# An attention and MLP kernel on one core: other homes for two PSUM banks, the gate inside V's product, four kinds of small work on GpSimd, and new planner values

## The chip, the core and the metric

The kernel runs on one core of a Trainium2 chip. A core has five engines that run their own instruction streams: TensorE (PE) multiplies matrices, VectorE (DVE), ScalarE (ACT) and GpSimd (POOL) work elementwise, and SyncE (SP) issues transfers. They wait for each other by semaphores. The metric is the device time of one execution in microseconds; the figure that counts is the median of several executions.

## The reference

x is 2048 x 512 in bfloat16. Two branches and a gate are computed from it:

```
g  = sigmoid((x * gate_w).sum(-1))
a  = attention of 32 heads of 16 columns (softmax over all 2048 keys) @ wo
h  = gelu(layernorm(x) @ w1), its four column quarters shifted by 1, -1, 2, -2 rows
x1 = x + h @ w2
b  = x1 + gelu(layernorm(x1) @ w3) @ w4          (w3: 512 x 1792)
out = g * a + (1 - g) * b
```

## The kernel before

**The planner.** The Python code that builds the kernel is a planner. It holds a clock for each of TensorE, ScalarE, VectorE and GpSimd (`free`), estimated durations, and queues of work that is ready at a planned time (`post`, `queue`). In its last loop it takes again and again the engine whose next piece can start first, chooses among that engine's pieces by rank, and issues the instruction. The order of instructions on each engine is thus fixed when the kernel is built; on the chip only the semaphores decide when each starts. Numbers such as CREDIT, SLACK and GAP and the table RULES (values for each unit of work, in place of those in USUAL) steer its choices.

**Attention.** A unit is one chunk of 512 queries and four heads: 4 chunks x 8 sets = 32 units of 64 score blocks (4 heads x 16 key tiles), each block 128 keys x 512 queries. A slot is three PSUM banks; two slots alternate. TensorE computes three blocks into a slot (`scores`, line 728), ScalarE takes the exponential of them in one instruction (`expo`, line 1036) into a tile `pt`, and TensorE multiplies these with V into the unit's sums `acc` (`attend`, line 1049). V has a column of ones, so the sums hold the softmax denominators too.

**Blocks without ScalarE.** Some blocks take another way. `wants_whole` decides whether the third bank of a slot (`dsc`) holds such a block. VectorE reads it from PSUM into an int16 tile with a shift and a floor (`dump`, line 927), so that the integers are the bits of a bfloat16 approximation of the exponential. Four blocks of one key tile make a group, 128 x 2048. Four further passes (`shifted`, line 964) add constants to the bits, and all five versions are multiplied with V and summed, which evens the approximation out. The group's tiles are called quad, more and xT after the memory they lie in. MAXD caps the blocks of a unit that go this way, CHAINS the groups under way, NEED says from how near the end of a unit the next unit's blocks are taken, and DLIM how much ready VectorE work forbids a new group. A slot without any exponential (`lone_slot`) can stand ahead of and behind a GELU round and holds up to three such blocks.

**The end of a unit.** `finish_unit` copies the sums to `accsb` (line 1119), sends the denominators through DRAM to spread them, and multiplies with their reciprocals (`scale`, line 1142). There is one `accsb`: the next unit's copy waits for the scaling.

**Jobs.** Between the slots TensorE runs jobs: projections of Q, K and V, the MLP's products and the output, in one PSUM bank (`psG`, tag gen) beside the unit's sums (`psA`, tag acc). A credit, raised with every slot, limits them. `q_proj` makes a unit pair's queries: the product is copied from PSUM into two versions, each with half of the columns set to zero by `mask` (line 287). `v_proj` makes half of V's heads for one key tile (copy in line 309), `gates` the gate's sums as one-column products (line 398). `norm` makes layernorm's normalised tiles (line 350). GELU rounds run on ScalarE and need another function table, so that tables are loaded twice for each round.

**Zero products.** Where TensorE would be idle for longer, `fill` multiplies a zero matrix into the open sums, which changes nothing in them.

**The start.** Lines 118 to 145 issue the first loads and prepare constants: GpSimd clears tiles and makes `ident`, `identf` and `minus`, VectorE sums `ident` to `mask` and scales it. Then x's first chunk is transposed on TensorE and copied to `xT` by VectorE and ScalarE (lines 1276 to 1284).

Of the kernel before, what the change touches and what calls it, by code (L numbers as in the profile page):

```python
# [32 lines left out]
def kernel(  # L33
# [21 lines left out]
    VK = 7  # L55
# [39 lines left out]
    wkv = wshare.tile([P, KT, 2 * D], BF16, tag="wshare", name="wkv")  # L95
# [11 lines left out]
    mask = const.tile([P, 2], F32, name="mask")  # L107
    pick = const.tile([P, 4], F32, name="pick")
# [33 lines left out]
    for a in range(2):  # L142
        nc.vector.tensor_reduce(out=mask[:, a:a + 1], in_=idv[:, a], op=ALU.add, axis=AX.XY)
    nc.vector.tensor_scalar(out=mask[:], in0=mask[:], scalar1=QS, scalar2=None, op0=ALU.mult)
# [7 lines left out]
    for j in range(4):  # L152
        for a in range(2):
# [8 lines left out]
    USUAL = {"NEED": 28, "AHEAD": 16, "HURRY": 14, "DLIM": 0.9, "MANY": 5, "PTS": 4, "CHAINS": 5, "MAXD": 16}  # L162
# [34 lines left out]
    state = {"n": 0, "gen": 0, "young": True, "mm": 0, "sp": 0.0, "before": True, "after": False, "aside": 0.0, "kind": "", "t": 0.0, "piece": 0.0,  # L197
             "credit": 0.0, "mixable": 0, "done": False, "ending": False, "acc": 0.0, "accsb": 0.0, "slot": 0, "outs": 0, "bank": 0}
    asides = deque()
    at = {}  # L200
    banks = {0: 0.0, 1: 0.0, 2: 0.0}

    port = {"vector": 0.0, "pool": 0.0}

    def dma(t, own, count=1):

        state["sp"] = max(state["sp"], t) + own * count
        return state["sp"]  # L210

    def post(engine, rank, cost, fn, ready=0.0, shared=False):

        state["n"] += 1
        queue[engine].append((rank, state["n"], cost, fn, ready, shared or engine == "pool"))

    def all_at(*keys):
        return lambda: max(at[k] for k in keys) if all(k in at for k in keys) else None

    def bank_of():
        return state["gen"] % 3 if state["young"] and state["slot"] < EARLY - 1 else 0

    def gen(name, dtype=F32):
        b = bank_of()
# [5 lines left out]
        return psG.tile([P, CH], dtype, tag="gen", name=name)  # L232
# [46 lines left out]
    def q_proj(c, G):  # L279
# [4 lines left out]
        def fn(end):  # L284
            qT = qpool.tile([P, 2, CH], BF16, tag="qT", name="qT")
            qTs[(c, G)] = qT
            nc.vector.tensor_tensor(out=qT[:], in0=ps[:].unsqueeze(1).to_broadcast([P, 2, CH]),
                                    in1=mask[:].unsqueeze(2).to_broadcast([P, 2, CH]), op=ALU.mult)
            at["q", c, G] = end

        evac(1.23, fn)
        yield MM

    def v_proj(t, half):
# [97 lines left out]
    def gates(c):  # L392
# [3 lines left out]
        for j in range(4):  # L396
# [4 lines left out]
            if j < 3:  # L401
                yield 0.2
# [345 lines left out]
    def scores(start):  # L748
# [21 lines left out]
        if mine:  # L770
            blocks = blocks[:2]
# [695 lines left out]
```

## Time and profile before

| | |
|---|---|
| median of 3 runs | 815.23 us (812.69 to 815.72) |
| the profiled execution | 814.83 us, its span 812.9 us |
| TensorE's mean granted clock | 0.987 |
| busy: PE, VectorE, ScalarE, GpSimd | 768.2, 739.5, 778.4, 16.5 us |

The span goes from the first to the last instruction. A row of a group view gives line, engine, operation, output and input tiles with their shapes and a count, then the busy time in us, the mean of one in ns, and the engine's idle time ahead of these instructions with what ended it. A row of a timeline gives start and duration in us. A row of waits gives the total in us, how often, and the longest.

### The profile page before, as it was taken

The numbers are of one execution on the slowest core, as the hardware profiler recorded it, in microseconds if no ns is written. First come the engines' busy times: TensorE is split into PE (matmuls) and PEld (weight loads), VectorE is DVE, ScalarE is ACT, GpSimd is POOL, SyncE is SP. The second block draws the span as 40 slices with busy tenths as digits, with TensorE's granted clock in tenths as the row PEclk, the third lists the DMA queues.
The fourth block names the chain that finished last, engine by engine and source line by source line (L and its number), as shares of the span: only waits on it lengthen the run. The fifth ranks groups of instructions, "written<-read, shape, count | busy, mean of one in ns | idle before, by whom it ended". The sixth has DMA issues, their size and how long they took to land.

```text
span 812.9 us, 24041 instructions
## 1 busy us (share of the span) xinstructions
PE 768.2 (95%) x10308; PEld 265.5 (33%) x10308; DVE 739.5 (91%) x1293; ACT 778.4 (96%) x726; POOL 16.5 (2%) x46
## 2 busy tenths in 40 slices
PE   8999999999999999989999999999999999999997
PEld 4333333233433333332333333333233333323333
DVE  5899989799689999998999997799987999999897
ACT  6999999999899999998999999999999999999996
POOL 3100000000000000000000000000000000000000
PEclk9999999799999999998999999999999999999999
DMA  9600033101200014000100011100020000000101
GB/s 191 193 20 15 11 77 33 44 19 41 44 5 18 17 59 91 9 18 15 43 14 13 25 39 31 29 9 16 19 57 16 8 31 17 23 19 19 31 13 40
DMA packets 52307, 29.05 MB, mean 36 GB/s; under 512 B 36713, under 2 KB 47721, under 8 KB 52201
## 3 DMA queue, kind: packets, MB, share of 16 engines
q1 hardware_dynamic: 51240, 27.00, 13.8%
q8 instruction: 80, 1.31, 0.7%
q10 hardware_dynamic: 960, 0.52, 0.2%
q14 instruction: 27, 0.21, 0.1%
HBM read 17.17 MB, written 2.35 MB: 24 GB/s over the span
## 4 chain that ended last, share of the span: by engine, by line
ACT 51%; PE 26%; issue 18%; DVE 4%; DMA 1%; POOL 1%; SPq 0%; DVEq 0%; ACTq 0%; POOLq 0%
ACT pt L1036 48%; PE acc L1049 10%; PE stage L728 7%; PE ps L237 2%; PE stage L237 2%; PE ps_y L237 1%; DVE quad L927 1%; PE acc L237 1%; ACT g2T L1014 1%; DMA xT<-in_A_x_dram 1%; ACT L1036 1%; ACT g2T L1017 1%; PE ps_q L237 1%; DVE quad L964 1%; PE ps_o L237 1%
## 5 line engine op out<-in xcount | busy, mean ns | idle before, releaser
L1036 ACT ACTIVATE pt<-stage 128x1024 bf16<-128x1024 f32 (+1 forms) x687 | 729.0, 1219 | 18.3 <-PE stage L728 13.6
L728 PE MATMUL stage<-qT,kT 32*128 32x512 bf16 (+2 forms) x1640 | 270.6, 382 | 32.7 <-ACT pt L1036 26.7
L927 DVE TENSOR_SCALAR quad<-dsc 128x512 int16<-128x512 f32 x300 | 200.5, 687 | 12.2 <-PE dsc L728 10.4
L728 PEld LDWEIGHTS <-kT 32*128 32x128 bf16 x2072 | 86.1, 91 | 275.7 <-issue 241.4
L964 DVE TENSOR_SCALAR quad<-quad 128x2048 int16<-128x2048 int16 x248 | 165.2, 685 | 4.5 <-PE acc L1049 4.2
L728 PE MATMUL dsc<-qT,kT 32*128 32x512 bf16 x432 | 165.9, 387 | 0.0
L1049 PE MATMUL acc<-pt,vp 128*17 128x512 bf16 (+3 forms) x1616 | 157.2, 383 | 3.3 <-DVE accsb L1119 2.7
L1049 PEld LDWEIGHTS <-vp 128*17 128x17 bf16 (+1 forms) x3896 | 86.1, 90 | 147.8 <-issue 109.2
L1049 PE MATMUL acc<-quad,vp 128*17 128x512 bf16 x1556 | 132.6, 388 | 0.3 <-DVE quad L964 0.2
L237 PE MATMUL ps<-w,g2T 128*32 128x512 bf16 x896 | 69.2, 381 | 0.0
L927 DVE TENSOR_SCALAR more<-dsc 128x512 int16<-128x512 f32 x79 | 52.7, 686 | 7.2 <-PE dsc L728 6.5
L237 PE MATMUL ps_y<-xnT,w 128*32 128x512 bf16 x704 | 55.1, 386 | 0.1
L237 PE MATMUL acc<-wq,zero 128*32 128x512 bf16 x596 | 51.1, 390 | 0.0
L237 PEld LDWEIGHTS <-w 128*32 128x32 bf16 x1152 | 29.3, 96 | 30.8 <-issue 12.9
L927 DVE TENSOR_SCALAR xT<-dsc 128x512 int16<-128x512 f32 x53 | 35.1, 686 | 2.7 <-PE dsc L728 2.3
L1049 PE MATMUL acc<-more,vp 128*17 128x512 bf16 x380 | 37.2, 388 | 0.1
L1049 PE MATMUL acc<-xT,vp 128*17 128x512 bf16 x344 | 32.6, 383 | 0.0
L964 DVE TENSOR_SCALAR more<-more 128x2048 int16<-128x2048 int16 x39 | 26.6, 685 | 1.5 <-PE acc L1049 1.4
L1119 DVE COPY accsb<-acc 128x512 f32<-128x512 f32 x31 | 21.3, 688 | 6.5 <-PE acc L1049 5.8
L237 PEld LDWEIGHTS <-g2T 128*32 128x32 bf16 x896 | 20.5, 95 | 19.9 <-issue 10.2
L237 PE MATMUL stage<-xnT,w 128*32 128x512 bf16 x448 | 25.1, 379 | 0.5 <-ACT pt L1036 0.5
L964 DVE TENSOR_SCALAR quad<-more 128x2048 int16<-128x2048 int16 x37 | 25.3, 687 | 0.1
(114 smaller groups left out, 543.2 us busy)
## 6 DMA issues: line engine op xcount, KB each, us to landing
bcs<-rec_d SPq DMA_DIRECT2D x31, 256.0 KB
w<-in_B_w_dram SPq DMA_DIRECT2D x2, 1792.0 KB
out_dram<-ot SPq DMA_DIRECT2D x15, 128.0 KB
x_sb<-in_A_x_dram SPq DMA_DIRECT2D x14, 128.0 KB
oT<-oT SPq DMA_DIRECT2D x112, 16.0 KB
w<-in_B_w_dram SPq DMA_DIRECT2D x2, 512.0 KB
wkv<-in_A_wqkv_dram SPq DMA_DIRECT2D x1, 512.0 KB
wo_all<-in_A_wo_dram SPq DMA_DIRECT2D x8, 64.0 KB
```

Source lines behind the costliest of these rows:

```text
L237: nc.tensor.matmul(out[j:j + 32, :], lhsT=lhsT[:, j:j + 32], rhs=rhs, tile_position=(0, j), **kwargs)
L728: nc.tensor.matmul(out, lhsT=kT[G][32 * j:32 * j + 32, cc, o:o + P], rhs=qTs[(c, G)][32 * j:32 * j + 32, a, lo:hi], start=True, stop=True, ...
L927: nc.vector.tensor_scalar(out=bits[:, r, :], in0=dsc[:], scalar1=SHIFT, scalar2=LOWEST, op0=ALU.add, op1=ALU.max)
L964: nc.vector.tensor_scalar(out=tiles[to], in0=tiles[base], scalar1=STEPS[i] - (STEPS[0] if base else 0.0), scalar2=None, op0=ALU.add)
L1014: nc.scalar.activation(out=part, in_=part, func=ACT.Gelu_apprx_tanh)
L1017: nc.scalar.activation(out=dst, in_=stages.pop(k)[:, 0:len(ms) * CH].rearrange("p (a c) -> p a c", c=CH), func=ACT.Gelu_apprx_tanh)
L1036: nc.scalar.activation(out=pt[:, 0:w], in_=stages.pop(k)[:, 0:w], func=ACT.Exp, scale=LN2 / 128.0)
L1049: nc.tensor.matmul(accs[n][32 * j:32 * j + M, lo:hi], lhsT=lhsT, rhs=p, start=(kt == 0), stop=(kt == NT - 1), skip_group_check=True, tile_ ...
L1119: nc.vector.tensor_copy(out=accsb[:], in_=acc[:])
```

## The change

Six things change. (1) The two banks for sums and for jobs lose their fixed roles: if the job bank is free earlier than the sums' bank, a new unit takes it and the roles are exchanged (`homes`, `swaps`). (2) The gate's weights become a 1025th column of the tile of K's and V's weights, written by GpSimd (`column`); the second half of V's product has 257 columns, and the last is the gate's sum. (3) A dump may take up to three neighbouring blocks (rule WIDE, and slots without an exponential). (4) On GpSimd now run: the two masked versions of the queries (with `ones`, in place of one VectorE pass), the normalised tiles, the scaling of all units but the last three, and the last of a group's four shifts where much VectorE work is ready (BACK). (5) The planner keeps account of TensorE's busy share over the last 3.4 us and adds zero products where it falls under 0.4 (`share`, LOW). (6) A tiny exponential behind each GELU round; values and RULES are new.

The diff, with the RULES, repeated entries of the account and lines that only pass on new arguments left out:

```diff
-    VK = 7
+    VK = 5
...
-    wkv = wshare.tile([P, KT, 2 * D], BF16, tag="wshare", name="wkv")
+    wkv = wshare.tile([P, KT, 2 * D + 1], BF16, tag="wshare", name="wkv")
...
+    ones = const.tile([P, 2], F32, name="ones")
+    small = const.tile([P, 1], F32, name="small")
...
+    nc.gpsimd.tensor_copy(out=ones[:], in_=mask[:])
...
-    USUAL = {"NEED": 28, "AHEAD": 16, "HURRY": 14, "DLIM": 0.9, "MANY": 5, "PTS": 4, "CHAINS": 5, "MAXD": 16}
+    USUAL = {"WIDE": 1, "NEED": 28, "AHEAD": 8, "HURRY": 24, "DLIM": 0.9, "MANY": 3, "PTS": 5, "CHAINS": 6, "MAXD": 16}
...
-    VLIM = 2.0
+    VLIM = 6.0
-    RUN = 9.5
+    LOOK = 0.3
+    BACK = 0.6
+    RUN = 1.5
-    CREDIT = 0.5
-    LATER = 0.4
-    GELU, WTWO = 1.2, 1.0
-    MOST = 16.0
+    CREDIT = 0.35
+    LATER = 0.35
+    GELU, WTWO = 1.0, 1.3
+    MOST = 12.0
-    SLACK = 0.3
-    GAP = 0.3
-    AGE = 2.0
-    ARANK = 3
+    SLACK = 0.25
+    GAP = 0.2
+    AGE = 4.0
+    ARANK = 4
-    TANH = 1.5
+    TANH = 3.0
+    WINDOW = 3.4
+    LOW = 0.4
+    PINCH = 0.2
...
+    busy = deque()
+    def works(a, b):
+        busy.append((a, b))
+        while busy[0][1] < b - 8.0:
+            busy.popleft()
+    def share(t):
+        return sum(min(b, t) - max(a, t - WINDOW) for a, b in busy if b > t - WINDOW) / WINDOW
...
+    homes = {"acc": (psA, "acc"), "gen": (psG, "gen")}
+    def home(kind, dtype, name):
+        pool, tag = homes[kind]
+        return pool.tile([P, CH], dtype, tag=tag, name=name)
...
-            nc.vector.tensor_tensor(out=qT[:], in0=ps[:].unsqueeze(1).to_broadcast([P, 2, CH]),
-                                    in1=mask[:].unsqueeze(2).to_broadcast([P, 2, CH]), op=ALU.mult)
-            at["q", c, G] = end
-        evac(1.23, fn)
+            nc.vector.tensor_scalar(out=qT[:, 0, :], in0=ps[:], scalar1=QS, scalar2=None, op0=ALU.mult)
+            def second(end):
+                nc.gpsimd.tensor_scalar(out=qT[:, 1, :], in0=qT[:, 0, :], scalar1=ones[:, 1:2], scalar2=None, op0=ALU.mult)
+                post("pool", 0, 0.65, first, end)
+            def first(end):
+                nc.gpsimd.tensor_scalar(out=qT[:, 0, :], in0=qT[:, 0, :], scalar1=ones[:, 0:1], scalar2=None, op0=ALU.mult)
+                at["q", c, G] = end
+            post("pool", 0, 0.65, second, end)
+        evac(0.69, fn)
-        yield all_at(("xT", c), "wv")
+        yield all_at(("xT", c), ("wv", half))
-            strips(ps[:, 0:width], lhsT=xT[c][:, kt, o:o + P], rhs=wkv[:, kt, D + half * width:D + (half + 1) * width],
-                             start=(kt == 0), stop=(kt == KT - 1))
+            strips(ps[:, 0:width + half], lhsT=xT[c][:, kt, o:o + P],
+                   rhs=wkv[:, kt, D + half * width:D + (half + 1) * width + half], start=(kt == 0), stop=(kt == KT - 1))
...
-        evac(0.42, fn)
+            if half:
+                nc.vector.tensor_copy(out=g_raw[:, t:t + 1], in_=ps[:, width:width + 1])
+                state["raw"] += 1
+                if state["raw"] == NT:
+                    post("act", 1, 0.1, tanh, end + 0.06)
+        evac(0.42 + 0.12 * half, fn)
...
-                nc.vector.tensor_scalar(out=xn[:], in0=x_sb[t][:], scalar1=mvs[n][:, t, 0:1],
+                nc.gpsimd.tensor_scalar(out=xn[:], in0=x_sb[t][:], scalar1=mvs[n][:, t, 0:1],
-            aside(0.41, normed(t), all_at(("rstd", n, c), "xnfree"), True)
+            post("pool", 1, 0.65, normed(t), all_at(("rstd", n, c), "xnfree"))
...
-    def gates(c):
-        yield all_at("gw", ("xT", c))
-        ps = gen("ps_g")
-        for j in range(4):
-            for kt in range(KT):
-                nc.tensor.matmul(ps[:, j:j + 1], lhsT=xT[c][:, kt, j * P:(j + 1) * P], rhs=gw[:, kt:kt + 1],
-                                 start=(kt == 0), stop=(kt == KT - 1))
-            state["piece"] += 0.2
-            if j < 3:
-                yield 0.2
-        def raw(end):
-            nc.vector.tensor_copy(out=g_raw[:, 4 * c:4 * c + 4], in_=ps[:, 0:4])
-            if c == NC_ - 1:
-                post("act", 1, 0.1, tanh, end + 0.06)
-        def tanh(end):
-            nc.scalar.activation(out=g_t[:], in_=g_raw[:], func=ACT.Tanh, scale=0.5)
-            post("vector", 5, 0.17, affine, end)
-        def affine(end):
-            nc.vector.tensor_scalar(out=g_fin[:], in0=g_t[:], scalar1=0.5, scalar2=0.5, op0=ALU.mult, op1=ALU.add)
-            at["g_fin"] = end
-        evac(0.2, raw)
-        yield 0.3
+    def tanh(end):
+        nc.scalar.activation(out=g_t[:], in_=g_raw[:], func=ACT.Tanh, scale=0.5)
+        post("vector", 5, 0.17, affine, end)
+    def affine(end):
+        nc.vector.tensor_scalar(out=g_fin[:], in0=g_t[:], scalar1=0.5, scalar2=0.5, op0=ALU.mult, op1=ALU.add)
+        at["g_fin"] = end
...
-    def wants_whole(blocks, now, alone=False):
+    def wants_whole(blocks, now, alone=0):
-        heads = {m % 4 for _, m in blocks[:2]}
+        most = alone or rule("WIDE")
+            most = min(most, len(rest))
+            heads = [m % 4 for _, m in blocks[:3 - most]]
-            if fit or k - quad["last"] > 2 or alone:
-                return n, kt, (fit or rest)[0]
+            if len(fit) >= most or k - quad["last"] > 2 or alone:
+                return n, kt, (fit + [j for j in rest if j in heads])[:most]
+        heads = [m % 4 for _, m in blocks[:3 - most]]
...
-                return n, kt, [j for j in range(4) if j not in heads][0]
+                last = heads[-1] if heads else 3
+                return n, kt, [j for j in ((last + d) % 4 for d in (1, 3, 2, 4)) if j not in heads][:most]
...
-        st = old[side].tile([P, (2 if kind else 3) * CH], F32, tag="stage", name="stage")
-        return st, old[side].tile([P, CH], F32, tag="dsc", name="dsc") if kind else None
+        st = old[side].tile([P, (3 - kind) * CH], F32, tag="stage", name="stage")
+        return st, old[side].tile([P, kind * CH], F32, tag="dsc", name="dsc") if kind else None
...
-            blocks = blocks[:2]
+            blocks = blocks[:3 - len(mine[2])]
-            st, dsc = stage(k, bool(mine))
+            st, dsc = stage(k, len(mine[2]) if mine else 0)
...
-        for i in range(3):
-            if i:
-                mine = wants_whole([], start, True)
-            if not mine:
-                break
-            n, kt, j = mine
+        i = 0
+        while mine:
+            n, kt, js = mine
-            rows[j] += 1
-            score(st[:, i * CH:(i + 1) * CH], n, 4 * kt + j)
-            whole(k, st[:, i * CH:(i + 1) * CH], n, kt, j, begin + (rows[j] - 1) * MM + PE_OUT)
+            for x, j in enumerate(js):
+                rows[j] += 1
+                score(st[:, (i + x) * CH:(i + x + 1) * CH], n, 4 * kt + j)
+            whole(k, st[:, i * CH:(i + len(js)) * CH], n, kt, js, begin + (max(rows) - 1) * MM + PE_OUT)
+            i += len(js)
+            mine = wants_whole([], start, 3 - i) if i < 3 else None
+        works(begin, free["pe"])
...
-            nc.vector.tensor_scalar(out=bits[:, r, :], in0=dsc[:], scalar1=SHIFT, scalar2=LOWEST,
+            nc.vector.tensor_scalar(out=bits[:, r:r + wide, :], in0=dsc.rearrange("p (a c) -> p a c", c=CH), scalar1=SHIFT, scalar2=LOWEST,
...
-            nc.vector.tensor_scalar(out=tiles[to], in0=tiles[base], scalar1=STEPS[i] - (STEPS[0] if base else 0.0), scalar2=None, op0=ALU.add)
+            shift = STEPS[i] - (STEPS[0] if base else 0.0)
+            if other:
+                nc.gpsimd.tensor_scalar(out=tiles[to], in0=tiles[base], scalar1=1.0, scalar2=shift, op0=ALU.mult, op1=ALU.add)
+            else:
+                nc.vector.tensor_scalar(out=tiles[to], in0=tiles[base], scalar1=shift, scalar2=None, op0=ALU.add)
...
-                post("vector", rank(), 0.69, lambda end: shifted(end, i + 1), end if i == 0 else room_or_base(i + 1, end), True)
+                work = sum(x[2] for x in queue["vector"] if not callable(x[4]) and x[4] < end + 1.0)
+                to_pool = i == 2 and work > BACK and free["pool"] < end + 1.0
+                state["pool"] = to_pool
+                post("pool" if to_pool else "vector", rank(), 2.0 if to_pool else 0.69, lambda end: shifted(end, i + 1, to_pool), end if i == 0 else room_or_base(i + 1, end), True)
...
-            free["act"] += LOAD
+            nc.scalar.activation(out=small[:], in_=mhalf[:, 0:1], func=ACT.Exp)
+            free["act"] += LOAD + 0.06
...
+    def swaps():
+        if current["job"] or banks[0] is None or state["moved"]:
+            return False
+        return state["acc"] is None or banks[0] < state["acc"] - 0.2
...
+                elif not accs and swaps():
+                    best = (max(t, banks[0]), waiting)
...
-                accs[n] = psA.tile([P, CH], F32, tag="acc", name="acc")
+                if swaps():
+                    homes["acc"], homes["gen"] = homes["gen"], homes["acc"]
+                    banks[0] = state["acc"]
+                    state["moved"] = state["acc"] is None
+                accs[n] = home("acc", F32, "acc")
...
-            state["acc"] = end
+            if state["moved"]:
+                banks[0], state["moved"] = end, False
+            else:
+                state["acc"] = end
...
-            post("vector", 0 if n >= len(units) - 3 else 3, 0.68, scale, lambda: landed if oroom or u % 2 else None, True)
+            late = n >= len(units) - 3
+            post("vector" if late else "pool", 0 if late else 3, 0.68 if late else 1.3, scale, lambda: landed if oroom or u % 2 else None, True)
-            nc.vector.tensor_tensor(out=oT, in0=tiles["accsb"][:], in1=tiles["bcs"][:], op=ALU.mult)
+            (nc.vector if n >= len(units) - 3 else nc.gpsimd).tensor_tensor(out=oT, in0=tiles["accsb"][:], in1=tiles["bcs"][:], op=ALU.mult)
...
-    at.update({("xT", 0): 0.0, ("xT", 1): 12.9, ("xT", 2): 15.5, ("xT", 3): 19.5, "wv": 10.5, ("wk", False): 0.0, ("wq", False): 0.0,
-               ("wk", True): 24.0, ("wq", True): 26.0, "gw": 28.0, ("q", 0, 0): 0.0, ("k", 0, 0): 0.0})
+    at.update({("xT", 0): 0.0, ("xT", 1): 12.9, ("xT", 2): 15.5, ("xT", 3): 19.5, ("wv", 0): 10.5, ("wk", False): 0.0, ("wq", False): 0.0,
+               ("wk", True): 24.0, ("wq", True): 26.0, ("q", 0, 0): 0.0, ("k", 0, 0): 0.0})
+    def column(end):
+        nc.gpsimd.tensor_copy(out=wkv[:, :, 2 * D], in_=gw[:])
+        at["wv", 1] = end
+    post("pool", 0, 0.1, column, 28.0)
...
-        if (soon > f + GAP and state["mm"] < quota or f + SLACK < soon < 1e8 and not state["young"]) and spare:
+        low = soon < 1e8 and not state["young"] and soon > f + PINCH and share(min(soon, f + 1.0)) < LOW
+        if (low or soon > f + GAP and state["mm"] < quota or f + SLACK < soon < 1e8 and not state["young"]) and spare:
```

More of the change, by code (lines that the diff above doesn't have):

```diff
@@ L902, in produce, with whole @@
         products.insert(i, (n, *term))
-    def whole(k, dsc, n, kt, j, ready):
+    def whole(k, dsc, n, kt, js, ready):
         if quad["open"] is None:
@@ L913, in whole @@
         bits, heads, rest, tiles = quad["tiles"], quad["heads"], quad["open"][2], {}
-        rest.remove(j)
-        r, full = len(heads), not rest
-        heads.append(j)
+        for j in js:
+            rest.remove(j)
+        r, wide, full = len(heads), len(js), not rest
+        heads.extend(js)
         if full:
@@ L945, in give, with shifted @@
             due[n] -= 1
-        def shifted(end, i):
+        def shifted(end, i, other=False):
             if i == 0:
```

39 lines of the change are left out of this document (23 added, 16 removed).

## The prediction

> **What bounds the kernel now.** I read the page first, then the groups by shape, then windows of 50 us, then the waits of ScalarE.
>
> ```profile
> span 812.9 us, 24041 instructions
> PE 768.2 (95%) x10308; PEld 265.5 (33%) x10308; DVE 739.5 (91%) x1293; ACT 778.4 (96%) x726; POOL 16.5 (2%) x46
> ```
> ```profile
> L1036 ACT ACTIVATE pt<-stage 128x1024 bf16<-128x1024 f32 x469 | 445.0, 1087 | 10.3 <-PE stage L728 6.3 <-PE dsc L728 3.0 <-ACT pt L1036 0.3
> L1036 ACT ACTIVATE pt<-stage 128x1536 bf16<-128x1536 f32 x218 | 305.5, 1505 | 8.0 <-PE stage L728 7.3 <-PE acc L1049 0.3
> ```
> ```profile
> 250.00:300.00 50.00, 47.00 (x618) 16.24 (x610) 49.02 (x87) 49.32 (x47) 1.98 (x2) 1.00 0.05 15
> 300.00:350.00 50.00, 46.62 (x596) 15.25 (x588) 49.62 (x88) 49.39 (x49) 1.01 (x1) 1.00 0.27 66
> 500.00:550.00 50.00, 48.53 (x697) 17.01 (x687) 40.96 (x69) 47.71 (x42) 0.00 (x0) 1.00 0.11 25
> ```
>
> ScalarE's exponentials fill the span, and VectorE, which takes some score blocks off ScalarE, is as full: the windows' columns are PE, weight loads, VectorE, ScalarE, GpSimd, then the clock. From 250 to 350 us VectorE has 98.6 of 100 us and ScalarE 98.7. TensorE looks as full, but 596 of its matmuls multiply zeros to keep its clock up (four of them run side by side), so it has room:
>
> ```profile
> L237 PE MATMUL acc<-wq,zero 128*32 128x512 bf16 x596 | 51.1, 390 | 0.0
> ```
>
> The two exponential rows give the exchange rate. They hold 2 x 469 + 3 x 218 = 1592 blocks of 128x512; the attention has 32 x 16 x 4 = 2048, so 456 blocks, 114 groups of four, go over VectorE. One block more or less in an exponential is 1505 - 1087 = 418 ns of ScalarE, a group 1.67 us. On VectorE a group is four dumps and four shifts:
>
> ```profile
> L927 DVE TENSOR_SCALAR quad<-dsc 128x512 int16<-128x512 f32 x300 | 200.5, 687 | 12.2 <-PE dsc L728 10.4
> L964 DVE TENSOR_SCALAR quad<-quad 128x2048 int16<-128x2048 int16 x248 | 165.2, 685 | 4.5 <-PE acc L1049 4.2
> ```
> ```profile
> 306.28 0.69 DVE L927 TENSOR_SCALAR quad<-dsc 128x512 int16<-128x512 f32 x1
> 306.88 0.69 DVE L964 TENSOR_SCALAR quad<-quad 128x2048 int16<-128x2048 int16 x1
> ```
>
> Neighbours start 0.60 us apart, 0.09 less than they last. So one instruction occupies 0.60 and a group 8 x 0.60 = 4.8 us. The time falls if VectorE is relieved of other work and takes groups instead, or if ScalarE's gaps close.
>
> **What leaves VectorE.** Each at its duration less 0.09.
>
> ```profile
> L1142 DVE TENSOR_TENSOR oT<-accsb,bcs 128x512 bf16<-128x512 f32 x31 | 21.3, 686 | 4.2 <-DMA bcs<-rec_d 4.2
> L350 DVE TENSOR_SCALAR xn<-x_sb,mv,rstd 128x512 bf16<-128x512 bf16 x32 | 12.3, 409 | 0.0
> L287 DVE TENSOR_TENSOR qT<-ps_q,mask 128x1024 bf16<-128x1024 f32 x15 | 18.2, 1216 | 1.0 <-PE ps_q L237 0.9
> L309 DVE CAST vp<-ps_v 128x256 bf16<-128x256 f32 x32 | 13.3, 414 | 2.8 <-PE ps_v L237 2.8
> L405 DVE COPY g_raw<-ps_g 128x4 f32<-128x4 f32 x4 | 0.6, 159 | 0.1
> ```
>
> - Unit scaling, 29 of 31 (the units from n = 29 on keep VectorE): 29 x 0.60 = 17.4 us.
> - Normalised tiles: 32 x 0.32 = 10.2 us.
> - Queries: 15 drop from 1.22 to one pass of 0.69, 15 x 0.53 = 8.0 us; the masking becomes two GpSimd passes.
> - The gate: four copies go, sixteen one-column copies come, each about the 159 ns of L405, less 0.09: 0.9 us more work. The 64 one-column matmuls go, which TensorE has room for anyway.
> - Wide dumps: the slot's rule WIDE is 1 in the usual values and in every unit's own, so ordinary slots dump one block as before. Only slots without an exponential use the new shape, three at once. L309 against L927 makes 256 columns 0.27 us and the rest 0.14; three blocks in one are 0.14 + 3 x 0.55 = 1.79, less 0.09, against 3 x 0.60: 0.1 saved each time. With at most two such slots for each of five GELU rounds that is 1 us, the whole of the wide dumps.
> - The last of a group's four shifts goes to GpSimd if over 0.6 us of VectorE work is ready. VectorE is full, so that often holds: 0 to 114 times, I take 60, 36 us.
>
> Sum: 17.4 + 10.2 + 8.0 - 0.9 + 1 + 36 = 72 us; bounds 36 and 104.
>
> **What GpSimd pays.**
>
> ```profile
> L1255 POOL TENSOR_TENSOR ot<-ot,parts 128x512 bf16<-128x512 f32 x1 | 1.3, 1266 | 426.4 <-DVE oT L1228 426.4
> L126 POOL MEMSET vp<- 128x1024 bf16 x1 | 1.0, 951 | 0.0
> L140 POOL TENSOR_SCALAR minus<-ident 128x128 bf16<-128x128 bf16 x1 | 0.5, 536 | 0.0
> ```
>
> The scaling has the form of L1255: 29 x 1.27 = 37 us. A 128x512 pass with one input isn't shown: it lies between L140's 0.54 for a quarter of it and 1.27 for two inputs; I take 0.7, near half of L126 plus a start, so 62 x 0.7 = 43 us. A 128x2048 shift lies between twice L126, 1.9, and four times L1255, 5.1; I take 2.1, as it has one input: 60 x 2.1 = 126 us. Together 206 us, a quarter of the span; at the upper ends 37 + 79 + 306 = 422, still half. Each is late, but off the path: queries are made a unit ahead (about 25 us; 1.4 us more here), and a unit's scaling must only precede the next unit's copy out of PSUM. If GpSimd's queue grew to a unit's length, that copy (L1119) and the next sums would wait.
>
> **What VectorE loses to GpSimd.** One row shows the two meeting:
>
> ```profile
> 249.05 0.69 DVE L964 TENSOR_SCALAR quad<-quad 128x2048 int16<-128x2048 int16 x1
> 249.22 1.38 POOL L340 TENSOR_TENSOR rstd<-rstd,mhalf 128x4 f32<-128x4 f32 x1 [215.28 <-DVE rstd L339]
> 343.54 0.69 DVE L373 CAST g2T<-ps_y 128x512 bf16<-128x512 f32 x1
> 343.71 1.01 POOL L340 TENSOR_TENSOR rstd<-rstd,mhalf 128x4 f32<-128x4 f32 x1 [45.20 <-DVE rstd L339]
> ```
>
> The same GpSimd instruction takes 1.01 us beside a VectorE read of PSUM and 1.38 beside a shift: it waits. The reverse isn't shown. With 30 + 32 + 29 + 60 = 151 GpSimd instructions, VectorE's loss is 0 if it never waits, and about half of 206, 103 us, if every one catches a shift halfway. The builder holds shifts until GpSimd's planned end and issues dumps, which read PSUM, meanwhile; so I take 0.13 us each, 20 us.
>
> **What ScalarE gets.** Three terms besides.
>
> ```profile
> L1036 ACT ACT_TABLE_LOAD x5 | 6.4, 1283 | 3.7 <-PE stage L728 2.6 <-PE dsc L728 1.0
> L410 ACT ACTIVATE g_t<-g_raw 128x16 f32<-128x16 f32 x1 | 0.4, 356 | 0.0
> ```
>
> - After each GELU round the table load now waits 3.7 us in all for the next scores. A tiny exponential issued at once makes the load run in that wait: -3.7, and five instructions like L410 at 0.27: +1.3. Net -2.4.
>
> ```profile
> 150.00:155.00 5.00, 4.81 (x38) 1.13 (x35) 4.54 (x8) 4.91 (x6) 0.00 (x0) 0.59 0.28 59
> 210.00:215.00 5.00, 5.00 (x65) 1.58 (x61) 4.26 (x7) 2.97 (x4) 0.00 (x0) 0.77 0.51 82
> 370.00:375.00 5.00, 5.00 (x66) 1.46 (x54) 4.30 (x9) 2.25 (x3) 0.00 (x0) 0.73 0.00 0
> ```
> ```profile
> ACT pt L1036 <- PE stage L728: 13.6, 16, 2.8
> ```
> ```profile
> PE acc L1049 <- DVE accsb L1119: 2.7, 7, 0.8
> ```
> ```profile
> 369.08 3.88 PE acc L1049 x36
> ```
>
> - ScalarE is idle for 2.03 us of 210 to 215 and 2.75 of 370 to 375. There the clock is down after thin use, and the chain of waits shows the rest: 36 product matmuls, 3.88 us, run in one go while ScalarE needs scores. The new account of TensorE's share puts zero products ahead of such stretches, RUN falls from 9.5 to 1.5 so that scores are considered after two groups of products, and the exchange of banks lets a unit start before the copy that costs TensorE 2.7 us. I take 6 of the 13.6 us; bounds 0 and 10 (the others are at the start).
> - The start loses. `ones`, copied from `mask` on GpSimd, stands in GpSimd's queue behind `minus`; the scaling of `mask` in place must then wait for that copy, and VectorE's copies of xT stand behind it:
>
> ```profile
> 6.44 0.54 POOL L140 TENSOR_SCALAR minus<-ident 128x128 bf16<-128x128 bf16 x1
> ```
> ```profile
> 1.86 0.51 DVE L144 TENSOR_SCALAR mask<-mask 128x2 f32<-128x2 f32 x1
> 4.77 1.32 DVE L1284 COPY xT<-ps_t 128x512 bf16<-128x512 bf16 x3 [2.41 <-PE ps_t L1280]
> ```
> ```profile
> 8.77 7.44 ACT L1036 ACTIVATE pt<-stage 128x1024 bf16<-128x1024 f32 x8 [0.93 <-PE stage L728]
> 16.84 143.70 ACT L1036 ACTIVATE pt<-stage 128x1024 bf16<-128x1024 f32 x137 [0.64 <-PE stage L728]
> ```
>
> `minus` ends at 6.98, the copy at about 7.1, `mask` at 7.65 instead of 2.37, and the xT copies start at about 7.7, 2.9 us late. The first exponential moves to 11.7. The wait of 0.64 at 16.84 (keys of the second chunk) swallows a part: +2.3, bounds 0 and 2.9.
>
> **The sum.** VectorE is busy 739.5 of 814.8 us, 0.91, and I leave it that share. With q groups more the time falls by 1.67 q + 2.4 + 6 - 2.3, and VectorE's room by 0.91 of that: 72 - 20 - 0.91 x 6.1 = (4.8 + 0.91 x 1.67) q, q = 46.4 / 6.3 = 7.4; I take 7, 11.7 us. TensorE pays four products of some 0.2 us more for each, 6 us, in place of zero products. Rules and credits for the single units only spread this: the caps MAXD add up to 528 blocks before and 520 after, above today's 456. The profiled execution took 814.83 us (its span 812.9), 0.4 under the median of 815.23: 814.8 - 11.7 - 2.4 - 6 + 2.3 = **797 us**.
>
> **The rivals.**
>
> 1. *VectorE waits for GpSimd* (slower). If a shift cannot start while a GpSimd instruction runs, and real times drift from the plan, each of the 151 costs a wait. Against it stand the builder's account and the dumps between; for it stands the 0.37 us in the other direction at 249 us. With 80 us lost (0.53 each): 739.5 - 72 + 7 x 4.8 + 80 = 781 us of work, and with 40 us of idle time, half of now's 75, 821 us. Late dumps hold PSUM, and ScalarE starves. With 55 us idle it decides from 760 us of work, a loss of about 60 us, 0.4 for each instruction. The Trainium skill, SBUF — State Buffer, section SBUF: two separate sides, says that the pair of ports is an exclusive lock that either engine can take from the other; by it this rival would be real on both sides, and the row at 249 us agrees on the one. The Trainium skill, GPSIMD Engine Reference, Engine selection, advises VectorE for elementwise work; by that the shifts above all should stay.
> 2. *The room isn't used* (no change). The groups stay at 114 because caps, tiles or the credits set them: 814.8 - 2.4 + 2.3, with no gap closed, 815 us. The gain for 500 to 550 us, where VectorE has 9 us of room unused, speaks for it; 250 to 350 against.
> 3. *The room is used in full.* All 104 us, no loss: (104 - 0.91 x 10.1) / 6.3 = 15 groups, 25 us, and 10 of gaps: 814.8 - 25 - 2.4 - 10 + 2.3 = 780 us. It needs 15 of the 16 groups that the caps leave above 456.
>
> **How the numbers follow.** Forecast 0.57, rival 1 0.22, rival 2 0.09, rival 3 0.12. A measurement of this kernel tells about 0.5%, 4 us, from no change. The forecast's own range is 786 to 809. The range goes from rival 3 to just past rival 1: 780 to 823. Faster: forecast and rival 3, 0.69, less 0.01 for its upper edge; same: rival 2, less a third on the slow side, and that edge, 0.08; slower: 0.24.
>
> **What would show it.** Right: over 456 blocks dumped, fewer 128x1536 exponentials and ScalarE's exponentials about 739 us; the GpSimd rows near 1.3, 0.7 and 2.1; shifts staying near 0.69; the first exponential near 11.7 us; zero products where the clock fell. Wrong: shifts well over 0.69 or gaps in VectorE released by GpSimd (rival 1), 456 blocks again (rival 2), or a first exponential still near 8.8.

## The result, and the profile after

The changed kernel takes 900.73 us (median of 4 runs, 896.67 to 907.52) against 813.96 us before: a ratio of 1.107 (95% interval 1.100 to 1.115), 87 us slower. The profiled execution took 907.52 us. The head of its page:

```profile
span 905.7 us, 24641 instructions
PE 816.6 (90%) x10503; PEld 255.1 (28%) x10504; DVE 785.0 (87%) x1204; ACT 778.1 (86%) x730; POOL 371.2 (41%) x226
```

No engine is full any more. ScalarE's busy time is what it was, spread over a span 93 us longer; VectorE, with 89 instructions fewer, is busy for 46 us more. A page also follows the chain of work that ended last back to the start, at each step to what released it. Its shares by engine, before and after ("issue" is time in which an engine waited for nothing that the profile shows, a q an engine's sequencer):

```profile
ACT 51%; PE 26%; issue 18%; DVE 4%; DMA 1%; POOL 1%; SPq 0%; DVEq 0%; ACTq 0%; POOLq 0%
```
```profile
DVE 41%; PE 38%; issue 8%; POOL 6%; ACT 5%; DMA 1%; SPq 1%; DVEq 0%; POOLq 0%; ACTq 0%
```

What ended the idle time shows where the engines stand. First two groups of before (the exponentials of both shapes, the products of the groups), then the changed kernel's (the exponentials, a VectorE dump, a VectorE shift, the products of the groups):

```profile
L1036 ACT ACTIVATE pt<-stage 128x1024 bf16<-128x1024 f32 (+1 forms) x687 | 729.0, 1219 | 18.3 <-PE stage L728 13.6
L1049 PE MATMUL acc<-quad,vp 128*17 128x512 bf16 x1556 | 132.6, 388 | 0.3 <-DVE quad L964 0.2
```

```profile
L1073 ACT ACTIVATE pt<-stage 128x1024 bf16<-128x1024 f32 (+1 forms) x686 | 728.0, 1169 | 109.6 <-PE dsc L751 69.7
L956 DVE TENSOR_SCALAR quad<-dsc 128x512 int16<-128x512 f32 x296 | 195.6, 681 | 26.5 <-PE dsc L751 25.0
L997 DVE TENSOR_SCALAR quad<-quad 128x2048 int16<-128x2048 int16 x221 | 202.0, 926 | 5.0 <-PE acc L1086 4.7
L1086 PE MATMUL acc<-quad,vp 128*17 128x512 bf16 x1668 | 148.8, 389 | 34.1 <-DVE quad L997 32.0
```

ScalarE waits 109.6 us for scores (before, 18.3). TensorE has not computed them, in good part because it stands in front of group products whose shift isn't done: 34.1 us of waiting in this row where it was 0.3, and 52 us in all rows of this kind together, 42 for VectorE's shifts and 10 for GpSimd's. And the shift is late because it lasts 926 ns where it lasted 685. The dumps, which read PSUM, keep their 0.68. Over all nine rows of that line, the durations of VectorE's 401 shifts add up to 367 us; at the 686 ns of before they would be 275. VectorE lost 92 us inside its own shifts. TensorE's mean granted clock was 0.951 where it was 0.987; in the kernel with short shifts (e2 below) it is 0.985 again, so it fell with the waits. How much of the 87 us is the clock's isn't separated here.

The new GpSimd rows:

```profile
L995 POOL TENSOR_SCALAR quad<-quad 128x2048 int16<-128x2048 int16 x54 | 113.1, 2097 | 166.7 <-PE acc L1086 137.9 <-DVE xT L956 13.6 <-DVE quad L956 7.0
L389 POOL TENSOR_SCALAR xn<-x_sb,mv,rstd 128x512 bf16<-128x512 bf16 x32 | 74.7, 2342 | 3.6 <-DMA xnT<-xn 3.3
L1195 POOL TENSOR_TENSOR oT<-accsb,bcs 128x512 bf16<-128x512 f32 x29 | 39.3, 1354 | 121.1 <-DMA bcs<-rec_d 54.5 <-issue 31.1 <-DVE quad L997 14.1
L316 POOL TENSOR_SCALAR qT<-qT,ones 128x512 bf16<-128x512 bf16 x15 | 29.9, 1992 | 88.5 <-DVE qT L313 88.5
```

And how the two engines meet, from the timelines of GpSimd and of VectorE (start, duration), first beside masked queries, then beside a group shift:

```profile
442.86 2.69 POOL L316 TENSOR_SCALAR qT<-qT,ones 128x512 bf16<-128x512 bf16 x1 [3.04 <-DVE qT L313]
...
601.80 2.33 POOL L995 TENSOR_SCALAR more<-more 128x2048 int16<-128x2048 int16 x1
```
```profile
442.85 0.62 DVE L997 TENSOR_SCALAR quad<-more 128x2048 int16<-128x2048 int16 x1
443.39 0.67 DVE L997 TENSOR_SCALAR more<-quad 128x2048 int16<-128x2048 int16 x1
443.99 1.09 DVE L997 TENSOR_SCALAR xT<-more 128x2048 int16<-128x2048 int16 x1
...
602.30 2.38 DVE L997 TENSOR_SCALAR quad<-more 128x2048 int16<-128x2048 int16 x1
604.60 0.67 DVE L997 TENSOR_SCALAR quad<-xT 128x2048 int16<-128x2048 int16 x1
```

GpSimd's shift ends at 604.13; VectorE's, begun at 602.30, ends at 604.68, half a microsecond later: it did its work after GpSimd's was over. This is no single case: of the 69 VectorE shifts in the trace that begin while a group shift runs, 66 end 0.54 to 0.64 us after that one's end. Beside the masked queries VectorE's shifts lose 0.4 us or nothing, and GpSimd's instruction grows from 2.0 to 2.7. Added over the trace, 81 of the 92 us lie beside a group shift on GpSimd (87 of them, so 0.9 us each), about 11 beside all its other work. The Trainium skill, SBUF — State Buffer, Who interferes with whom, says of a VectorE instruction in a 2-port mode and a GpSimd instruction that whichever engine issues first holds the shared ports for its whole instruction and the other is blocked. The trace doesn't give the shifts' mode; by that rule the trace agrees for the group shifts (2.38 us) and not for the bfloat16 instructions (0.67 and 1.09 for two shifts that begin inside one of 2.69).

### The profile page after: what moved, and what is told of

It reads as the page before. It is cut to its first block, busy times and chain, and to the rows that moved or that the text cites. A ratio compares the mean times of both kernels' runs of the same rounds, so it can differ in the third digit from the quotient of the medians.

```text
span 905.7 us, 24641 instructions
## 1 busy us (share of the span) xinstructions
PE 816.6 (90%) x10503; PEld 255.1 (28%) x10504; DVE 785.0 (87%) x1204; ACT 778.1 (86%) x730; POOL 371.2 (41%) x226
## 4 chain that ended last, share of the span: by engine, by line
DVE 41%; PE 38%; issue 8%; POOL 6%; ACT 5%; DMA 1%; SPq 1%; DVEq 0%; POOLq 0%; ACTq 0%
DVE quad L997 13%; PE acc L1086 12%; PE stage L751 10%; DVE quad L956 9%; ACT pt L1073 5%; DVE more L997 3%; PE ps L263 3%; DVE more L956 3%; DVE xT L997 3%; DVE xT L956 3%; PE stage L263 3%; PE ps_y L263 2%; PE acc L263 2%; POOL xn L389 2%; DVE accsb L1168 1%
## 5 line engine op out<-in xcount | busy, mean ns | idle before, releaser
L1073 ACT ACTIVATE pt<-stage 128x1024 bf16<-128x1024 f32 (+1 forms) x686 | 728.0, 1169 | 109.6 <-PE dsc L751 69.7
L751 PE MATMUL stage<-qT,kT 32*128 32x512 bf16 (+1 forms) x1611 | 278.9, 391 | 10.5 <-ACT pt L1073 5.7
L997 DVE TENSOR_SCALAR quad<-quad 128x2048 int16<-128x2048 int16 x221 | 202.0, 926 | 5.0 <-PE acc L1086 4.7
L751 PE MATMUL dsc<-qT,kT 32*128 32x512 bf16 x461 | 184.1, 399 | 10.8 <-DVE quad L956 6.3
L995 POOL TENSOR_SCALAR quad<-quad 128x2048 int16<-128x2048 int16 x54 | 113.1, 2097 | 166.7 <-PE acc L1086 137.9
L1086 PE MATMUL acc<-quad,vp 128*17 128x512 bf16 x1668 | 148.8, 389 | 34.1 <-DVE quad L997 32.0
L1195 POOL TENSOR_TENSOR oT<-accsb,bcs 128x512 bf16<-128x512 f32 x29 | 39.3, 1354 | 121.1 <-DMA bcs<-rec_d 54.5
L389 POOL TENSOR_SCALAR xn<-x_sb,mv,rstd 128x512 bf16<-128x512 bf16 x32 | 74.7, 2342 | 3.6 <-DMA xnT<-xn 3.3
L316 POOL TENSOR_SCALAR qT<-qT,ones 128x512 bf16<-128x512 bf16 x15 | 29.9, 1992 | 88.5 <-DVE qT L313 88.5
L995 POOL TENSOR_SCALAR xT<-xT 128x2048 int16<-128x2048 int16 x18 | 37.5, 2086 | 39.8 <-PE acc L1086 37.2
L995 POOL TENSOR_SCALAR more<-more 128x2048 int16<-128x2048 int16 x13 | 28.1, 2159 | 53.6 <-PE acc L1086 53.6
```

Of the source, the lines that this page charges most:

```text
L316: nc.gpsimd.tensor_scalar(out=qT[:, 1, :], in0=qT[:, 0, :], scalar1=ones[:, 1:2], scalar2=None, op0=ALU.mult)
L389: nc.gpsimd.tensor_scalar(out=xn[:], in0=x_sb[t][:], scalar1=mvs[n][:, t, 0:1], scalar2=rstds[n][:, t:t + 1], op0=ALU.subtract, op1=ALU.mult)
L751: nc.tensor.matmul(out, lhsT=kT[G][32 * j:32 * j + 32, cc, o:o + P], rhs=qTs[(c, G)][32 * j:32 * j + 32, a, lo:hi], start=True, stop=True, ...
L995: nc.gpsimd.tensor_scalar(out=tiles[to], in0=tiles[base], scalar1=1.0, scalar2=shift, op0=ALU.mult, op1=ALU.add)
L997: nc.vector.tensor_scalar(out=tiles[to], in0=tiles[base], scalar1=shift, scalar2=None, op0=ALU.add)
L1073: nc.scalar.activation(out=pt[:, 0:w], in_=stages.pop(k)[:, 0:w], func=ACT.Exp, scale=LN2 / 128.0)
```

## The experiments

Three theories were told apart. Theory 1: VectorE's shifts wait behind GpSimd's group shifts. Theory 2: the queries and tiles, which take 2 us and not the planned 0.65, come late. Theory 3: the rest of the change costs the time. Where an edit leaves the planner's numbers alone, every engine keeps the changed kernel's order; where it alters them, the whole plan is made anew. The short instructions leave work out: e2, e4, e19 and e20 shift 64 of a group's 2048 columns on GpSimd, and e3, e4, e9 and e19 neither mask the queries nor normalise the tiles. Their times test a cause; they aren't times of a kernel that could be used. In each table row, before was run on the same chip (812.5 to 814.2 us).

| kernel | plan | us | ratio to before, 95% |
|---|---|---|---|
| e1, shifts back on VectorE | new | 856.47 | 1.041 to 1.060 |
| e2, short GpSimd shift | same | 817.57 | 1.002 to 1.008 |
| e3, numbers for tile scalars | same | 891.64 | 1.086 to 1.102 |
| e4, e2 and e3 | same | 816.13 | 0.999 to 1.008 |
| e9, short queries and tiles | same | 882.22 | 1.073 to 1.095 |
| e5, true prices in the plan | new | 901.90 | 1.103 to 1.113 |
| e13, GpSimd shift in four | same | 855.85 | 1.047 to 1.060 |
| e14, before with GpSimd shifts | new | 900.82 | 1.102 to 1.116 |
| e8, shifts, queries, tiles back | new | 851.89 | 1.044 to 1.050 |
| e11, all back, old values | new | 906.82 | 1.110 to 1.118 |
| e16, before, table load early | new | 835.32 | 1.022 to 1.035 |
| e18, the same, plan kept | before's | 808.63 | 0.992 to 0.998 |
| e19, all GpSimd work short | same | 806.28 | 0.989 to 0.996 |
| e20, e2 with ones on VectorE | same | 817.16 | 1.004 to 1.009 |

**The group shifts, kept in place and made short (e2), or taken back (e1).**

```diff
-                nc.gpsimd.tensor_scalar(out=tiles[to], in0=tiles[base], ...
+                nc.gpsimd.tensor_scalar(out=tiles[to][:, :, 0:16], in0=tiles[base][:, :, 0:16], ...      (e2)
-                to_pool = i == 2 and work > BACK and free["pool"] < end + 1.0
+                to_pool = False                                                                        (e1)
```

> The plan and every engine's order are those of the changed kernel; only GpSimd's group shift writes 64 of its 2048 columns, so that it ends early (the other columns keep what the tile held). Theory 1: VectorE's shifts at about 0.70 us and the time 815-845. Theory 2: 870-900, since queries and normalised tiles still take 2 us. Theory 3: 870-900.

> All group shifts are on VectorE again, the other GpSimd work stays; the planner plans anew. Theory 1 (VectorE's shifts wait behind GpSimd's 2.1 us group shifts; 80 of the 89 us by which VectorE's shifts of the changed kernel are longer lie beside these): VectorE's shifts return to a mean of 0.69 to 0.72 us and the time falls from 901 to 815-840. Theory 2 (the masked queries and normalised tiles take 2 us on GpSimd and come late, and the engines stand waiting for them): 870-900. Theory 3 (the banks, the new planner values or the rest of the change cost the time): 870-900, with shifts at 0.69.

With the same order on every engine, the short shift gives back 83 of the 87 us. The groups of e2:

```profile
L1073 ACT ACTIVATE pt<-stage 128x1024 bf16<-128x1024 f32 (+1 forms) x686 | 718.1, 1195 | 36.0 <-PE dsc L751 19.1 <-PE stage L751 8.6 <-PE acc L1086 5.7
...
L997 DVE TENSOR_SCALAR quad<-quad 128x2048 int16<-128x2048 int16 x221 | 157.1, 723 | 6.6 <-PE acc L1086 6.3
```

VectorE's shifts are back at 723 ns and ScalarE's wait falls from 109.6 to 36.0 us: Theory 1. In e1 the shifts in quad take 717 ns, but its time, with the plan made anew, lay above its expectation, which left a second cost to be found.

**The price of queries and tiles (e3, e4, e9, e5).** In e3 the masks, means and deviations become numbers in the instruction; in e9 the instructions become int16 copies; e4 is e2 and e3 together; e5 tells the planner 2.0 and 2.1 us.

```diff
-                nc.gpsimd.tensor_scalar(out=qT[:, 1, :], in0=qT[:, 0, :], scalar1=ones[:, 1:2], ...
+                nc.gpsimd.tensor_scalar(out=qT[:, 1, :], in0=qT[:, 0, :], scalar1=1.0, ...               (e3)
+                nc.gpsimd.tensor_scalar(out=qT[:, 1, :].bitcast(I16), in0=qT[:, 0, :].bitcast(I16), scalar1=1.0, scalar2=0.0, ...   (e9)
-            post("pool", 1, 0.65, normed(t), all_at(("rstd", n, c), "xnfree"))
+            post("pool", 1, 2.1, normed(t), all_at(("rstd", n, c), "xnfree"))                        (e5)
```

> The plan and the order are those of the changed kernel; the masks and the mean and deviation are replaced by constant numbers in the instruction (queries unmasked, tiles only scaled), in place of values read from a tile. If reading the scalars from a tile is what makes these GpSimd instructions last 2 us, they fall to 0.6-0.8 us. Theory 1: the time stays at 875-900. Theory 2: 815-845. Theory 3: 870-900.

> Both at once, in the same plan: GpSimd's group shift over 64 columns and constant numbers in place of the tile scalars, so that GpSimd's work is about as short as planned or shorter. Theories 1 and 2: the plan is met and the time is 780-825, below the better of the two single ones. Theory 3: over 850 all the same, with VectorE's shifts at 0.69.

> Plan and order of the changed kernel, GpSimd's group shifts at full length. GpSimd's instructions for queries and normalised tiles become int16 copies of the same tiles (queries unmasked, tiles not normalised), which should take 0.5-0.7 us, near the 0.65 that the plan holds for them. Theory 1a (the plan's price of 0.65 for what takes 2 us makes GpSimd late, and only so do its group shifts meet VectorE's): 815-850, with VectorE's shifts at 0.70-0.75. Theory 1b (the group shifts meet VectorE's even where GpSimd's prices hold): 865-895, with VectorE's shifts still at 0.85 or more.

> The changed kernel with only the plan's prices set to what was measured: 2.0 us for each masked query pass, 2.1 for a normalised tile, in place of 0.65; the planner plans anew. Theory 1a: 820-860. Theory 1b: 870-905.

e3 missed its aim: with plain numbers the tiles still took 2.15 us and the queries 1.79, so it didn't test the price; 892 us says only that tile scalars aren't the cause, and e4 (816) repeats e2. e9 did:

```profile
L389 POOL TENSOR_SCALAR xn<-x_sb 128x512 int16<-128x512 int16 x32 | 23.9, 769 | 3.6 <-DMA xnT<-xn 3.5
L316 POOL TENSOR_SCALAR qT<-qT 128x512 int16<-128x512 int16 x15 | 12.7, 844 | 86.9 <-DVE qT L313 86.9
```

Near the planned price of 0.65, the kernel still takes 882 us and VectorE's shifts in quad a mean of 932 ns; the shorter instructions are worth 19 of the 87 us, but the collisions stay. A plan with the true prices (e5) takes 902. So the collisions don't come from mispriced instructions (theory 1b of the expectations, against 1a).

**Is it one instruction at a time? Are the shifts enough alone? (e13, e14)**

```diff
-                nc.gpsimd.tensor_scalar(out=tiles[to], in0=tiles[base], scalar1=1.0, scalar2=shift, ...
+                for x in range(4):
+                    nc.gpsimd.tensor_scalar(out=tiles[to][:, x, :], in0=tiles[base][:, x, :], scalar1=1.0, scalar2=shift, ...    (e13)
```

> Plan and order of the changed kernel; each GpSimd group shift is issued as four instructions of 512 columns, about 0.6 us each, with the same result. Theory 1b with waits for one GpSimd instruction at a time: a VectorE shift that meets it waits for the piece that runs, at most 0.6 us, not for 2.1; VectorE's shifts fall from a mean of 0.91 to 0.72-0.80 us and the time from 901 to 835-870. Rival (the waits come from GpSimd's total time, whatever its pieces): 890-920.

> The kernel before with one part of the change alone: the last shift of a group goes to GpSimd by the changed kernel's rule, and the plan, made anew, ends within 5 us of that of the kernel before. Theory 1b: 860-900, and VectorE's shifts at a mean of 0.85 us or more. Rival (the shifts harm only together with the other parts): 805-835.

Four pieces of about 0.76 us are 3.0 us of GpSimd in place of 2.1, and yet the time falls by 45 us. VectorE's row of e13:

```profile
L998 DVE TENSOR_SCALAR quad<-quad 128x2048 int16<-128x2048 int16 x221 | 177.8, 816 | 4.2 <-PE acc L1087 3.9
```

A shift that meets a piece waits for that piece: the longest beside one takes 1.24 us, where beside a whole group shift it was 2.42. For these int16 shifts what counts is the length of the single GpSimd instruction, not GpSimd's total time; the mean of 816 lay just over the expected 800. e14 is the kernel before with nothing but the choice of engine for the last shift, and loses all of the 87 us: 900.8, with a plan that ends only 5 us later. Its rows:

```profile
L1042 ACT ACTIVATE pt<-stage 128x1024 bf16<-128x1024 f32 (+1 forms) x687 | 730.5, 1177 | 96.5 <-PE dsc L728 52.7 <-PE stage L728 37.6 <-PE acc L1055 4.3
...
L968 DVE TENSOR_SCALAR quad<-quad 128x2048 int16<-128x2048 int16 x209 | 183.4, 888 | 4.0 <-PE acc L1055 3.9
...
L1055 PE MATMUL acc<-quad,vp 128*17 128x512 bf16 x1624 | 144.6, 395 | 32.5 <-DVE quad L968 32.2
```

**What remains when work is taken back (e8, e11, e16, e18).** e8 puts shifts, queries and tiles back on VectorE. e11 puts the scaling back too, with the old USUAL and RULES. e16 is the kernel before with the tiny exponential and its 0.06 us in the plan; e18 is the same without the 0.06.

```diff
+            nc.scalar.activation(out=small[:], in_=mhalf[:, 0:1], func=ACT.Exp)
-            free["act"] += LOAD
+            free["act"] += LOAD + 0.06         (e16 only)
```

> Group shifts, masked queries and normalised tiles on VectorE again, only the scaling of units stays on GpSimd; planned anew. Theory 2 (in the kernel with only the shifts back, 856 us, ScalarE's stands of 3 to 10 us come from normalised tiles and queries that are late): 805-830, no stand of ScalarE over 3 us. Theory 3 (banks, values and rules cost the time): 840 or more.

> Nothing of the change's elementwise work on GpSimd, and the values of USUAL and RULES as before; banks, gate column, wide dumps, the account of TensorE's share and the other planner values as changed. Theories 1 and 2: the rest of the change is worth little, 805-822. Theory 3: 840 or more.

> The kernel before with the tiny exponential behind each GELU round, for which the planner counts 0.06 us; this alters the plan from the first GELU round on, and the altered plan ends 21 us later by the planner's own clocks. Theory 3b (the values and RULES fit one plan; any other plan with the same values is some 20 us longer, whatever the part does): 825-840. Rival (the values are robust; the parts that are put back explain the 852 and 856 us): 808-815.

> The kernel before, its plan and order unchanged, with the tiny exponential behind each GELU round that the planner does not count. If the table loads then run while ScalarE waits for scores: 3.7 us of waiting less, five instructions of 0.2 us more: 809-812 where the kernel before takes 812-814. Rival (the wait only moves to the next exponential): 813-815.

e8 stayed at 852, with stands of ScalarE of up to 7.6 us and one of 18.6 at the end, and e11 went to 907: both lie where their expectations had theory 3. The planner's own clocks explain most of it. These are planned ends, not times of the chip:

```
                  planned end   measured   difference
before                790.3       814.0        24
e16                   811.7       835.3        24
e11                   875.0       906.8        32
e8                    813.9       851.9        38
e1                    797.5       856.5        59
e13                   772.3       855.9        84
e5                    807.7       901.9        94
e14                   795.3       900.8       106
after                 772.3       900.7       128
```

A plan without work on GpSimd, or with the scaling alone, ends 24 to 38 us after its planned end; with group shifts on GpSimd it is 84 to 128. In the plan of after (772.3) the difference is 128 with whole group shifts, 84 with pieces (e13), 45 with short ones (e2) and 34 with all new GpSimd work but the scaling short (e19). In e16, 0.06 us behind each of five GELU rounds makes the plan 21 us longer, and the chip follows by just as much (835.3). The values and RULES fit one plan; an altered number gives another, here 5 (e14) to 42 us (e8) longer than the one it was made from, and e16 shows that the edit need not be worth that. e11, old values under the new planner, is the extreme: 103. So e1, e8 and e11 say little about their parts. What makes e1's difference 59 stays open; queries and tiles of 2 us on GpSimd, which e8 (38) hasn't, are a candidate. With the order kept, e18 shows what the early table load is worth:

```profile
L1038 ACT ACTIVATE pt<-stage 128x1024 bf16<-128x1024 f32 (+1 forms) x687 | 728.2, 1221 | 16.3 <-PE stage L729 11.3 <-PE dsc L729 3.8 <-PE acc L1051 0.3
...
L1023 ACT ACT_TABLE_LOAD x5 | 6.4, 1283 | 0.1
```

The load's wait falls from 3.7 to 0.1 us, and the kernel takes 808.6 us (ratio 0.9949, interval 0.9921 to 0.9977). That is faster than before and after, and the kernel does all the work. The rows give a saving of 2.6 us: 3.6 of waiting less, and 1.0 for the five tiny exponentials. The medians differ by 5 because the time of either kernel also goes with TensorE's granted clock: on that chip before took 816.3 us in five runs at 0.985 and 808.7 in two at 1.000. In runs with the same clock of 0.993, three of each kernel, e18 takes 808.6 and before 811.4 us, 2.8 less. Whether the edit has a part in the slightly higher mean clock of its runs (0.994 against 0.991) isn't shown.

**Where the expected gain went (e19, e20).**

```diff
-    nc.gpsimd.tensor_copy(out=ones[:], in_=mask[:])
+    nc.vector.tensor_copy(out=ones[:], in_=mask[:])       (e20: with e2; e19: with e2 and e9)
```

> Plan and order of the changed kernel with all of GpSimd's new work short: group shifts over 64 columns, int16 copies in place of masked queries and normalised tiles, and the copy to ones on VectorE, so that the start doesn't wait for GpSimd. Only the scaling of units keeps its length. If the forecast's sum holds wherever GpSimd costs nothing: 790-802. Theory 3 (the other parts gave nothing; ScalarE's gaps stay): 808-818.

> The kernel with group shifts over 64 columns (817.6 us), and the copy to ones on VectorE. If the start costs what the first exponential shows (12.7 us in place of 8.8, less the 0.6 of waiting that it hides): the first exponential near 9 us, 812-816. Rival (the late start is hidden later): 816-819.

e19 came in between the two expectations: 806.3 us. Its exponentials:

```profile
L1072 ACT ACTIVATE pt<-stage 128x1024 bf16<-128x1024 f32 (+1 forms) x686 | 715.8, 1202 | 26.8 <-PE dsc L750 10.4 <-PE stage L750 8.3 <-PE acc L1085 6.5
```

The exponentials fell from 729.0 us on the page of before to 715.8, 13.2 less, but ScalarE's wait for scores grew from 18.3 to 26.8 us, 8.5 more; with 2.6 for the table loads that makes 7.3 of gain, and 6.3 was measured. In e20 the first exponential is back at 9.6 us from 12.7, and the time is the same as that of e2 (817.2 and 817.6): the late start doesn't show in it.

## Why the prediction was wrong, step by step

- **The step that failed: what VectorE loses to GpSimd.** The sum put 20 us, 0.13 us for each GpSimd instruction, since the builder holds shifts back until GpSimd's planned end. Measured: 92 us, 81 of them beside the 87 group shifts, 0.9 us for each. Rival 1 had the mechanism, nearly the loss (80) and VectorE's work (781 us against 785 measured); its time of 821 us fell short by 80 because it let VectorE's idle time shrink to 40 us. It grew to 121. With VectorE's share held at 0.91, as in the main sum, the rival's 781 us would have made 858. Nor is the size of the loss the whole failure: with 92 in place of 20, the sum's own rule gives (72 - 92 - 5.6) / 6.3, four groups fewer, and 815 us, not 901. It treats a loss as room on VectorE that fewer groups give back. But the groups and the orders are fixed when the kernel is built: a shift that is up to 2 us late stops TensorE at the product that needs it (32.0 us in the largest row), TensorE then doesn't compute the next scores, ScalarE stands (69.7 us for the third bank's scores), and VectorE gets its next dumps late (25.0 where it was 10.4). e2 and e13 show this by length in the same order, e14 by the part alone.
- **The builder's account.** It was taken as a shield. It knows planned times only, and the chip drifts from them: the plan ends at 772 us, the chip at 901. Where the drift begins wasn't traced; that the shield fails even with true prices is shown (e5, e9).
- **GpSimd's prices.** Scaling 1.27, measured 1.35; group shifts 2.1, measured 2.1, and 87 of them (54, 18, 13, 1 and 1 by tiles) where 60 were taken. Queries and tiles 0.7, measured 2.0 and 2.3, outside the stated bounds of 0.54 and 1.27. The quoted row of `minus` held the answer: 536 ns for 128 bfloat16 columns, four times which is 2.1. A two-input float32 row was no upper bound for another type. With short shifts this cost about 11 us: e2 with short queries and tiles and the copy moved (e19) goes from 817.6 to 806.3, and the copy alone gives nothing (e20). With the long shifts in place it was 19 (e9).
- **VectorE's relief and the groups.** 488 blocks went over VectorE, 122 groups, 8 more than before (7 forecast), and in e19 the exponentials lost 13.2 us (11.7 forecast): right, where the collisions are away. Rival 3 misread the caps: unit 0 takes no such blocks and the last unit's cap is 20, which makes 512 blocks before and after, room for 14 groups and not for its 15.
- **The gaps.** 6 us less of ScalarE's waits was forecast; without the collisions they are 8.5 us more (e19). Neither the account of TensorE's share (740 zero products where there were 596) nor the banks closed them in this plan. Which of the new rules opened others wasn't tried.
- **The start.** `mask` waited for GpSimd as foreseen (VectorE's wait of 5.3 us there, the first exponential at 12.7 us against 11.7 forecast), but the 2.3 us of the sum didn't show in the time: with the copy on VectorE the first exponential starts at 9.6 and the time is the same (e20).
- **Table loads.** Net -2.4 forecast; the wait fell by 3.6 and the tiny exponentials took 1.0 us, and e18 took 2.8 us less than before at the same clock: right.
- **Wide dumps.** Nine only, eight of three blocks at 1.75 us (rows of the groups by shape) and one of two; ordinary slots dumped single blocks: right.

## What to carry to other kernels

Work moved to GpSimd isn't free because GpSimd has time: look first at what one of its instructions makes VectorE wait (here up to 1.7 us beside an int16 pass of 2.1 us, 0.4 beside bfloat16 passes as long), and try it in pieces before its total is counted. In a kernel whose order is fixed beforehand, a late result can stop every engine behind it, as 92 us lost on VectorE became 87 us of the kernel here although VectorE had 75 us idle, so a loss on a nearly full engine should be carried through to the engine that feeds the bound one. Where values are fitted to one plan, test a part in an unchanged order (a shorter instruction at the same place), since every edit that the planner sees alters far more than the part.

## What the runs showed of the hardware

- On GpSimd the type sets the price: a one-input pass over 128x512 took 1.8 to 2.3 us in bfloat16, with scalars from a tile (after) or in the instruction (e3), and 0.74 to 0.84 us in int16 (e9, e19); 128x2048 in int16 took 2.1.
- GpSimd's bfloat16 passes, though as long, delayed VectorE's shifts by at most 0.4 us, while its int16 group shifts delayed them by up to 1.7 and its scaling (two inputs, float32 to bfloat16, 1.35 us) by up to 1.1. Why they differ is open.
